# A Fourier and gated-MLP block on one core: the first 512 rows of x and of their DFT blocks loaded in another token order

## The chip, the cores and the metric

The kernel runs on one core of a Trainium2 chip. TensorE (PE) multiplies matrices, VectorE (DVE), ScalarE (ACT) and GpSimd (POOL) work element by element, and SyncE (SP) mostly issues DMAs. ACT and POOL issue some as well. All share the core's 16 DMA engines. The metric is the time of one execution in microseconds (us), lower is better.

## The reference

x is 2048 tokens by 512 features. Only the first half matters for the change: a normalization of x, and a two-dimensional discrete Fourier transform written as products with given cosine and sine matrices, of which the real part is kept. Everything is float32.

```python
h = _layernorm(x, axis=-1) * (1 + ca) + sa
a = jnp.einsum("bsd,ed->bse", h, dft_hid_re)
b = jnp.einsum("bsd,ed->bse", h, dft_hid_im)
y = jnp.einsum("ts,bse->bte", dft_seq_re, a) - jnp.einsum("ts,bse->bte", dft_seq_im, b)
x = x + ga * y
h = _layernorm(x, axis=-1) * (1 + cb) + sb
x = x + gb * _B_ref(h, ...)        # gelu, layernorm, a product over tokens, a gate, an output product
```

## The kernel before

A float32 product is made of three fast products. Each operand is split into a high part and a low part (`ah` and `al` for the DFT, `hh` and `hl` for the normalized x). ACT writes the high part, DVE the difference, and PE multiplies high by high, high by low and low by high into one accumulator.

The first phase takes the sum over the tokens s of the sequence DFT before the product with the hidden DFT. It runs 128 steps, numbered n, of 12 matmuls (128x512) each. A step contracts 128 tokens: its weights are the four 128-column chunks of one tile of normalized x, its moving operand is T[n], a 128x512 tile that has tokens on the partitions and DFT rows t on the columns. The DFT matrices are cut into 32 blocks of 512x512 (`src`). Four steps share a block. For the first 512 rows t the blocks alternate between cosine and sine (n 0 to 3 cosine, 4 to 7 sine, on the same four x tiles). Row group g means tokens 512g to 512g+511, held as four tiles in `XG[g]`.

A block arrives in the buffer `stage` (two buffers) with DFT rows on the partitions. `squares` (L190) makes T[n] of it with DVE's transpose of 32x32 squares. Such a transpose moves a token only within its 32, so `load_block` (L155) puts four pieces of 128 columns on the four quarters of the partitions, one DMA of 32 partitions and 256 KB for each. Tile k of a row group thus consists of the tokens 128a + 32k + i (a = 0 to 3, i = 0 to 31), and x is loaded in that same order by four DMAs of 32 partitions.

Later steps run ahead by a plan: before step n, `prep(n)` makes T[n+3] and its high part, and the low part of step n+2. When a block's last T is made, the block after the next is loaded into its buffer. `at(n, f)` runs f after step n. SP issues nearly all loads in program order, and each DMA waits for the DMA eight before it in the ring of eight completion semaphores.

The start is written out by hand, and the change lies there:

- `keep_busy` (L369) gives PE three matmuls on constants (six recorded passes), so that it works from 1.5 us on.
- `load_two` and `load_half` load x tiles 0 and 1 and the first 64 columns of each quarter of block 0 (T[0] and T[1]), on SP and ACT at once. `load_x` and `load_half` bring x tiles 2 and 3 and the other 64 columns on SP, and `load(1)` the sine block.
- Step 0 multiplies unsplit float32 (`whole_first` makes `xn`, `turn_whole` T[0], L543). It reads the four chunks in the order 1, 2, 3, 0.
- Steps 1 to 3 (L549) need `hh` (L483), `ah` (L269), `al` (L287) and `hl` (L525). `stats_first` (L439 to L445) gives the statistics on DVE and POOL. `norm_x` (L121) writes the float32 x from which `hl` is made.
- T has two buffers: T[2] takes the place of T[0], which PE reads until step 0 ends.
- Step 4 is the first with the plan's order (L97, L98, L99 for high-high, high by `al`, `hl` by high).

Of the kernel before, what the change touches and what calls it, by code (L numbers as in the profile page):

```python
# [20 lines left out]
def fnet_gmlp_kernel(  # L21
# [32 lines left out]
    nc = tc.nc  # L54
    S, D = x.shape[1:]
    F2 = w_in.shape[1]
    FH = F2 // 2
    Q = 512
    NQ = S // Q
# [73 lines left out]
    def quad(a, r, k):  # L133
        return a[r * Q:(r + 1) * Q, k * Q:(k + 1) * Q]

    src = []
    for t in range(NQ):
        for g, j in ([(g, j) for g in range(NQ) for j in range(2)] if t == 0 else
                     [(g, j) for j in range(2) for g in range(NQ)]):
            src.append(quad((cr, ci)[j], t, g))  # L140
    N2 = 4 * len(src)
    N1 = N2 + 8
    YPROD = (6, 7, 4, 5, 3)
# [8 lines left out]
    def load_block(tile_, a, s0=0, s1=P):  # L152
        v = a.rearrange("(b j) (a s) -> a j b s", j=32, a=4)
        for q in range(4):
            nc.sync.dma_start(tile_[32 * q:32 * q + 32, :, s0:s1], v[q][:, :, s0:s1])  # L155

    def load_half(tile_, a, h, engs=(nc.sync,) * 4):

        v = a.rearrange("(b j) (a s) -> a j b s", j=32, a=4)
        for q in range(4):  # L160
            engs[q].dma_start(tile_[32 * q:32 * q + 32], v[q][:, :, 64 * h:64 * h + 64])

    XB = []

    def load(b):
        if b < len(src):
            stage[b] = blocks.tile([P, 16, P], F32, tag="stage", bufs=2, name=f"stage{b}")
            load_block(stage[b], src[b])
        elif b < len(src) + 2:
            j = b - len(src)  # L170
            XB.append(blocks.tile([P, 4, Q], F32, tag="stage", bufs=2, name=f"xb{j}"))
            for g in range(2):
                nc.sync.dma_start(XB[j][:, 2 * g:2 * g + 2], ht_d[g].rearrange("(k p) t -> p k t", p=P)[:, 2 * j:2 * j + 2])
                for kk in range(2):
                    TT[2 * j + kk, g] = XB[j][:, 2 * g + kk]
# [13 lines left out]
    def squares(dst, block, k):  # L189
        nc.vector.transpose(dst.rearrange("p (b i) -> p b i", i=32), block[:, :, 32 * k:32 * k + 32])  # L190
# [61 lines left out]
    def prep_hi(n):  # L252
        if n >= NE or n in highs:
            return
        highs.add(n)
        if N2 <= n < N4:
            T[n] = form_t(n)
        else:
            b, k = divmod(n, 4) if n < N2 else (NB0 + (n - N4) // 4, (n - N4) % 4)
            if b != NB0:  # L260
                T[n] = blocks.tile([P, Q], F32, tag="t", bufs=2, name=f"t{n}")
            if b == NB0:
                assert n in T
            elif n >= N4:
                squares(T[n], stage[b][:, k % 2], k // 2)
            else:
                squares(T[n], stage[b], k)
        AH[n] = SE[2][:, n - N4] if N4 <= n < N4 + 4 else blocks.tile([P, Q], F32R, tag="ah", bufs=4, name=f"ah{n}")
        nc.scalar.activation(AH[n], T[n], AF.Copy)  # L269
        if not N2 <= n < N4 and k == 3:  # L270
            stage.pop(b)
            if b != NB0:
                load(b + 2)


# [89 lines left out]
    def keep_busy(n, k):  # L365

        ps = bank(k, "busyp")
        for _ in range(n):
            nc.tensor.matmul(ps, ones, busy, start=True, stop=True)  # L369

    def fold_sum(t, w, u):

# [46 lines left out]

    X, XG, LN, NRM, h_hi, h_lo = {}, {}, {}, {}, {}, {}  # L420

    def load_x(g, ks=range(4), eng=nc.sync):

        if g not in XG:
            XG[g] = spool.tile([P, 4, D], F32, tag="x", bufs=2, name=f"x{g}")
        k0, k1 = ks[0], ks[-1] + 1
        v = x.rearrange("(g a k i) d -> g a i k d", g=NQ, a=4, i=32)
        for a in range(4):
            eng.dma_start(XG[g][32 * a:32 * a + 32, k0:k1, :], v[g, a][:, k0:k1, :])
        for k in ks:  # L430
            X[4 * g + k] = XG[g][:, k, :]

# [2 lines left out]

    def stats_first(s):

        m = spool.tile([P, 12], F32, tag="first", bufs=4, name=f"first{s}")
        nc.vector.bn_stats(m[:, :6], X[s])  # L439
        mv = m[:, 8:]  # L440
        nc.vector.bn_aggr(mv[:, :2], m[:, :6])
        nc.vector.tensor_scalar(mv[:, 1:2], mv[:, 1:2], EPS, None, op0=ALU.add)
        nc.gpsimd.tensor_tensor(mv[:, 2:3], mv[:, 1:2], mhalf, op=ALU.pow)
        eng = nc.gpsimd if s else nc.vector
        eng.tensor_scalar(mv[:, 3:4], mv[:, 0:1], mv[:, 2:3], -1.0, op0=ALU.mult, op1=ALU.mult)  # L445
        NRM[s] = mv[:, 2:3], mv[:, 3:4]

    two = (nc.sync, nc.sync, nc.scalar, nc.scalar)

    def load_two(k):  # L450
        if not k:
            XG[0] = spool.tile([P, 4, D], F32, tag="x", bufs=2, name="x0")
        v = x.rearrange("(g a k i) d -> g a i k d", g=NQ, a=4, i=32)
        for a in range(4):
            two[a].dma_start(XG[0][32 * a:32 * a + 32, k, :], v[0, a][:, k, :])
        X[k] = XG[0][:, k, :]

    def whole_first(s):

        LN[s] = spool.tile([P, D], F32, tag="xn", bufs=4, name=f"xn{s}")  # L460
        nc.scalar.activation(LN[s].rearrange("p (k a i) -> p k a i", a=4, i=32),
                             X[s].rearrange("p (a k i) -> p k a i", a=4, i=32), AF.Identity,
                             bias=NRM[s][1], scale=NRM[s][0])
        nc.scalar.activation(LN[s][:, :1], ones[:, :1], AF.Copy)

    def split_first(s):
# [6 lines left out]

    def turn_whole(n):
        T[n] = blocks.tile([P, Q], F32, tag="t", bufs=2, name=f"t{n}")
        squares(T[n], stage[0], n)
        highs.add(n)
        lows.add(n)

    def hi_first(s):  # L480
        h_hi[s] = hpool.tile([P, ND, P], F32R, name=f"hh{s}")
        h = h_hi[s].rearrange("p k (a i) -> p k a i", i=32)
        nc.scalar.activation(h, X[s].rearrange("p (a k i) -> p k a i", a=4, i=32), AF.Identity,  # L483
                             bias=NRM[s][1], scale=NRM[s][0])
        nc.scalar.activation(h_hi[s][:, 0, :1], ones[:, :1], AF.Copy)
# [20 lines left out]
    def norm_x(s):  # L506

        if s not in LN:
            ones_x(s)
        elif s > 3:  # L510
            nc.gpsimd.memset(LN[s][:, 0:1], 1.0)
        apply(LN[s][:, 1:], X.pop(s)[:, 1:], NRM.pop(s))
# [9 lines left out]
    def lo_h(s):  # L522
        h_lo[s] = hpool.tile([P, ND, P], F32R, name=f"hl{s}")
        lo, h = parts_h(s, h_lo)
        nc.vector.tensor_tensor(lo, h, parts_h(s, h_hi)[0].bitcast(F32), op=ALU.subtract)  # L525
        LN.pop(s)
# [557 lines left out]
            mm([n])  # L1084


    load_two(0)
    stage[0] = blocks.tile([P, 16, P], F32, tag="stage", bufs=2, name="stage0")
    load_half(stage[0][:, :, :64], src[0], 0, two)
    load_two(1)  # L1090
    nc.scalar.activation(sc, ones[:, :ND], AF.Silu)
    load_x(0, range(2, 4))
    load_half(stage[0][:, :, 64:], src[0], 1)
    load(1)
    load_x(1, range(2))
    keep_busy(3, 5)
    ones_x(1)
    ones_x(2)
    ones_x(3)
    stats_first(0)  # L1100
    whole_first(0)
    turn_whole(0)
    prep_hi(1)
    stats_first(1)
    prep_lo(1)
    hi_first(1)
    stats_first(2)
    norm_x(1)
    stats_first(3)
    hi_first(2)  # L1110
    lo_h(1)
    prep_hi(2)
    norm_x(2)
    prep_hi(3)
    prep_lo(2)
    lo_h(2)
    hi_first(3)
    norm_x(3)
    prep_lo(3)
    split_first(0)  # L1120
# [11 lines left out]
    for s, n in ((4, 4), (5, 4), (6, 6), (7, 6), (8, 10), (9, 10)):  # L1132
        m = n + (s == 9)
# [316 lines left out]
```

## Time and profile before

| | |
|---|---|
| median of 3 runs | 931.55 us (931.38 to 931.88) |
| the profiled execution | 931.77 us |
| its span from first to last instruction | 930.0 us |
| PE busy | 924.2 us, 99% of the span |
| DVE, ACT, POOL busy | 738.2, 409.1, 199.1 us |
| moved by DMA | 157.88 MB, mean 170 GB/s |
| granted TensorE clock, mean | 0.999 |

A timeline row gives the start, the duration, the engine, the line, what is written from what, the count, and in brackets the idle time just before it and what ended that. Rows of several instructions are merged. Ends of matmuls are modelled, so starts are the better guide. "SPq" rows are the issuing of DMAs by SP.

### The profile page before, as it was taken

What the parts mean: (1) busy time and instruction counts of PE and PEld (TensorE: products, weight loads), DVE (VectorE), ACT (ScalarE), POOL (GpSimd) and SP (SyncE); (2) the same over time, 40 slices, a digit from 0 to 9 for tenths busy, and PEclk for the clock granted to TensorE, in tenths of its full rate; (3) what the DMA queues carried; (4) which work ended last, traced back from release to release, by engine and by line L of the source; (5) the groups of instructions that cost most, each with busy time, mean ns of one, the idle gap of its engine ahead of it and who ended that gap; (6) DMA issues with size and microseconds to landing.
All of it is one profiled execution on the core that took longest, in us unless ns stands there. A gap on an engine that the chain in (4) does not pass through costs nothing.

```text
span 930.0 us, 12339 instructions
## 1 busy us (share of the span) xinstructions
PE 924.2 (99%) x4053; PEld 760.4 (82%) x4053; DVE 738.2 (79%) x1218; ACT 409.1 (44%) x733; POOL 199.1 (21%) x375
## 2 busy tenths in 40 slices
PE   9999999999999999999999999999999999999998
PEld 5888888888888888888888888888888888888887
DVE  7799968787687677875678788899799789986762
ACT  5694424232132222322577877674544544331121
POOL 2330000224554165323512321331000000000000
PEclk9999999999999999999999999999999999999999
DMA  9995762856639977996463864444464566734651
GB/s 218 225 227 118 142 158 46 193 147 171 158 91 319 283 220 217 275 343 227 141 217 130 279 201 103 118 105 105 105 146 102 130 142 143 178 97 149 185 178 57
DMA packets 246976, 157.88 MB, mean 170 GB/s; under 512 B 140384, under 2 KB 214368, under 8 KB 246784
## 3 DMA queue, kind: packets, MB, share of 16 engines
q1 hardware_dynamic: 233248, 119.57, 52.2%
q0 software_dynamic: 12272, 36.86, 11.4%
q8 instruction: 32, 0.52, 0.2%
q10 hardware_dynamic: 1392, 0.66, 0.2%
q14 instruction: 32, 0.26, 0.1%
HBM read 120.33 MB, written 36.71 MB: 169 GB/s over the span
## 4 chain that ended last, share of the span: by engine, by line
PE 98%; DMA 1%; SPq 0%; ACTq 0%; DVE 0%; ACT 0%; issue 0%; DVEq 0%
PE gp L99 12%; PE gp L97 12%; PE gp L98 12%; PE gw L99 10%; PE gw L97 10%; PE gw L98 10%; PE yp L99 3%; PE yp L98 3%; PE yp L97 3%; PE op L98 3%; PE op L97 3%; PE op L99 3%; PE fp L98 1%; PE fp L97 1%; PE fp L99 1%; PE z2s L98 1%
## 5 line engine op out<-in xcount | busy, mean ns | idle before, releaser
L269 ACT ACTIVATE ah<-t 128x512 fp32r<-128x512 f32 x235 | 148.5, 632 | 362.6 <-DVE t L190 242.7
L287 DVE TENSOR_TENSOR al<-t,ah 128x512 fp32r<-128x512 f32 x235 | 160.6, 683 | 55.7 <-PE gp L98 30.9
L98 PE MATMUL gp<-al,hh 128*128 128x512 f32 x496 | 193.0, 389 | 0.0
L97 PE MATMUL gp<-ah,hh 128*128 128x512 f32 x496 | 193.0, 389 | 0.0
L99 PE MATMUL gp<-ah,hl 128*128 128x512 f32 x496 | 193.0, 389 | 0.0
L190 DVE STREAM_TRANSPOSE t<-stage 128x512 f32<-128x512 f32 x236 | 165.5, 702 | 6.3 <-DMA stage<-in_A_dft_seq_re_dram 3.1
L98 PE MATMUL gw<-al,bh 128*128 128x512 f32 x400 | 155.6, 389 | 0.0
L99 PE MATMUL gw<-ah,bl 128*128 128x512 f32 x384 | 149.5, 389 | 0.0
L97 PE MATMUL gw<-ah,bh 128*128 128x512 f32 x384 | 149.4, 389 | 0.0
L98 PEld LDWEIGHTS gp<-al,hh 128*128 128x128 f32 x496 | 93.1, 188 | 19.5 <-DVE al L287 0.2
L97 PEld LDWEIGHTS gp<-ah,hh 128*128 128x128 f32 x496 | 93.1, 188 | 19.4
L99 PEld LDWEIGHTS gp<-ah,hl 128*128 128x128 f32 x496 | 93.1, 188 | 19.3
L98 PEld LDWEIGHTS gw<-al,bh 128*128 128x128 f32 x400 | 75.1, 188 | 15.7
L99 PEld LDWEIGHTS gw<-ah,bl 128*128 128x128 f32 x384 | 72.1, 188 | 15.3 <-DVE bl L948 0.3
L97 PEld LDWEIGHTS gw<-ah,bh 128*128 128x128 f32 x384 | 72.1, 188 | 14.9
L920 POOL DMA_DIRECT2D s_d<-sj x64 | 35.1, 548 | 107.2 <-DVE sj L912 82.3
L97 PE MATMUL yp<-hth,gh 128*128 128x512 f32 x128 | 49.8, 389 | 0.0
L98 PE MATMUL yp<-htl,gh 128*128 128x512 f32 x128 | 49.8, 389 | 0.0
L99 PE MATMUL yp<-hth,gl 128*128 128x512 f32 x128 | 49.8, 389 | 0.0
L665 POOL DMA_DIRECT2D ht_d<-hturn x62 | 41.0, 667 | 23.1 <-DVE hturn L661 18.2
L97 PE MATMUL op<-woh,uh 128*128 128x512 f32 x110 | 42.8, 389 | 0.0
L98 PE MATMUL op<-wol,uh 128*128 128x512 f32 x110 | 42.8, 389 | 0.0
(247 smaller groups left out, 1449.4 us busy)
## 6 DMA issues: line engine op xcount, KB each, us to landing
stage<-in_A_dft_seq_im_dram SPq DMA_DIRECT2D x64, 256.0 KB, 6.0
sj<-in_B_w_sp_dram SPq DMA_DIRECT2D x32, 512.0 KB, 7.2
s_d<-sj POOLq DMA_DIRECT2D x64, 256.0 KB, 4.7
stage<-s_d SPq DMA_DIRECT2D x128, 128.0 KB, 2.9
stage<-in_A_dft_seq_re_dram SPq DMA_DIRECT2D x60, 256.0 KB, 5.6
stage<-in_B_w_sp_dram SPq DMA_DIRECT2D x88, 128.0 KB, 3.0
wm<-in_w_mod_dram SPq DMA_DIRECT2D x16, 256.0 KB, 6.1
xr<-in_A_x_dram POOLq DMA_DIRECT2D x16, 256.0 KB, 4.5
```

Source lines behind the costliest of these rows:

```text
L97: nc.tensor.matmul(acc, ah, bh, start=first, stop=False, skip_group_check=go_on)
L98: nc.tensor.matmul(acc, ah, bl, start=False, stop=False, skip_group_check=go_on)
L99: nc.tensor.matmul(acc, al, bh, start=False, stop=last, skip_group_check=go_on)
L190: nc.vector.transpose(dst.rearrange("p (b i) -> p b i", i=32), block[:, :, 32 * k:32 * k + 32])
L269: nc.scalar.activation(AH[n], T[n], AF.Copy)
L287: nc.vector.tensor_tensor(AL[n], t, AH[n].bitcast(F32), op=ALU.subtract)
L665: eng.dma_start(v[a, i], ht[32 * a:32 * a + 32].rearrange("c (b r) -> c b r", r=32))
L920: nc.gpsimd.dma_start(s_d[m, r, g][b * P:(b + 1) * P, :], a)
```

## The change

Row group 0 gets another token order. Tiles 0 and 1 are tokens 0 to 127 and 128 to 255 in their own order: x for each is one DMA of 128 partitions and 256 KB. Tiles 2 and 3 are the even and odd tokens of 256 to 511: x for both is one DMA of 512 KB, 4 KB for each partition.

The DFT blocks whose columns are row group 0 (8 of the 32) follow. For each of tiles 0 and 1, `load_row_of` issues four DMAs of 64 KB, in pieces of 32 columns, 128 bytes. For tiles 2 and 3 together `load_pair` issues four DMAs of 128 KB in pieces of 256 bytes. Such a block takes 12 DMAs where it took 4. `turn_dft` transposes tiles 2 and 3 from every second column. The other 24 blocks and row groups keep their loads.

At the start ACT now issues four DMAs, quarters 2 and 3 of the pieces for T[0] and T[1]. `keep_busy` does the same three matmuls. `whole_first` is two ACT instructions, chunks 1 and 2 and then 0 and 3, and the last statistics step of tile 0 moves from DVE to POOL. The calls after it stand in another order.

```diff
+    def load_row_of(tile_, a, k, qs=range(4), eng=nc.sync):
+        v = a[:, k * P:(k + 1) * P].rearrange("(b j) (a s) -> a j b s", j=32, a=4)
+        for q in qs:
+            eng.dma_start(tile_[32 * q:32 * q + 32, :, 32 * k:32 * k + 32], v[q])
+
+    def load_pair(tile_, a):
+        v = a[:, 2 * P:].rearrange("(b j) (a s) -> a j b s", j=32, a=4)
+        for q in range(4):
+            nc.sync.dma_start(tile_[32 * q:32 * q + 32, :, 64:], v[q])
+
+    def turn_dft(n, block, k, bs=slice(0, 16)):
+        t = T[n].rearrange("p (b i) -> p b i", i=32)
+        if SRC_G[n // 4] or k < 2:
+            nc.vector.transpose(t[:, bs, :], block[:, bs, 32 * k:32 * k + 32])
+        else:
+            v = block.rearrange("p b (h i c) -> p b h i c", h=2, c=2)
+            nc.vector.transpose(t[:, bs, :], v[:, bs, 1, :, k - 2])
...
-            load_block(stage[b], src[b])
+            if SRC_G[b]:
+                load_block(stage[b], src[b])
+            else:
+                load_row_of(stage[b], src[b], 0)
+                load_row_of(stage[b], src[b], 1)
+                load_pair(stage[b], src[b])
...
+        if not g:
+            if k0 < 2:
+                nc.sync.dma_start(XG[g][:, k0, :], x[k0 * P:(k0 + 1) * P, :])
+            else:
+                nc.sync.dma_start(XG[g][:, 2:, :], x[2 * P:Q, :].rearrange("(p k) d -> p k d", k=2))
...
-    load_two(0)
+    load_x(0, range(1))
     stage[0] = blocks.tile([P, 16, P], F32, tag="stage", bufs=2, name="stage0")
-    load_half(stage[0][:, :, :64], src[0], 0, two)
-    load_two(1)
+    load_row_of(stage[0], src[0], 0, range(2))
+    load_row_of(stage[0], src[0], 0, range(2, 4), nc.scalar)
+    load_x(0, range(1, 2))
+    load_row_of(stage[0], src[0], 1, range(2, 4), nc.scalar)
+    load_row_of(stage[0], src[0], 1, range(2))
     nc.scalar.activation(sc, ones[:, :ND], AF.Silu)
     load_x(0, range(2, 4))
-    load_half(stage[0][:, :, 64:], src[0], 1)
+    load_pair(stage[0], src[0])
...
-    keep_busy(3, 5)
+    keep_busy((Q, Q, Q), 5)
...
     turn_whole(0)
+    stats_first(1)
     prep_hi(1)
-    stats_first(1)
-    prep_lo(1)
     hi_first(1)
     stats_first(2)
+    prep_lo(1)
     norm_x(1)
+    hi_first(2)
+    prep_hi(2)
+    lo_h(1)
     stats_first(3)
-    hi_first(2)
-    lo_h(1)
-    prep_hi(2)
     norm_x(2)
+    prep_lo(2)
     prep_hi(3)
-    prep_lo(2)
+    hi_first(3)
     lo_h(2)
-    hi_first(3)
     norm_x(3)
     prep_lo(3)
```

The order on DVE before, from the statistics of x tile 2 to the second transpose of block 1. `t_225` and `t_230` are T[2] and T[3], `t_268` is T[4], `al_239` the low part of step 2, `hl_223` that of x tile 1:

```order
L439 BN_STATS first_207<-x_138 128x6
...
L439 BN_STATS first_214<-x_138 128x6
L441 BN_AGGR first_214<-first_214 128x2
L442 TENSOR_SCALAR first_214<-first_214 128x1
L525 TENSOR_TENSOR hl_223<-xn_175,hh_204 128x512
L190 STREAM_TRANSPOSE t_225<-stage_143 128x512
L190 STREAM_TRANSPOSE t_230<-stage_143 128x512
L287 TENSOR_TENSOR al_239<-t_225,ah_227 128x512
L525 TENSOR_TENSOR hl_241<-xn_177,hh_220 128x512
L287 TENSOR_TENSOR al_247<-t_230,ah_232 128x512
L525 TENSOR_TENSOR hl_253<-xn_179,hh_243 128x512
L190 STREAM_TRANSPOSE t_268<-stage_161 128x512
```

The same place now, where `t_221` and `t_236` are T[2] and T[3], `hl_225` the low part of x tile 1 and `t_272` is T[4]:

```order
L314 TENSOR_TENSOR al_215<-t_202,ah_204 128x512
L183 STREAM_TRANSPOSE t_221<-stage_140 128x512
L560 TENSOR_TENSOR hl_225<-xn_178,hh_206 128x512
L476 BN_STATS first_227<-x_138 128x6
L481 BN_AGGR first_227<-first_227 128x2
L482 TENSOR_SCALAR first_227<-first_227 128x1
L314 TENSOR_TENSOR al_234<-t_221,ah_223 128x512
L183 STREAM_TRANSPOSE t_236<-stage_140 128x512
L560 TENSOR_TENSOR hl_248<-xn_180,hh_218 128x512
L314 TENSOR_TENSOR al_251<-t_236,ah_238 128x512
L560 TENSOR_TENSOR hl_257<-xn_182,hh_245 128x512
L180 STREAM_TRANSPOSE t_272<-stage_156 128x512
```

T[2] now stands ahead of `hl` of tile 1 and of the statistics of tile 3, and T[3] no longer follows T[2] directly: four kinds of work lie between them.

SP's queue before, down to the first ordinary block (`stage_143` is block 0, `stage_161` block 1, `stage_234` block 2):

```order
L455 DMA x_138<-in_A_x_dram 32x512 x2
L161 DMA stage_143<-in_A_dft_seq_re_dram 32x16x64 x2
L455 DMA x_138<-in_A_x_dram 32x512 x2
L429 DMA x_138<-in_A_x_dram 32x2x512 x4
L161 DMA stage_143<-in_A_dft_seq_re_dram 32x16x64 x4
L155 DMA stage_161<-in_A_dft_seq_im_dram 32x16x128 x4
L429 DMA x_166<-in_A_x_dram 32x2x512 x4
L155 DMA stage_234<-in_A_dft_seq_re_dram 32x16x128 x4
```

And now (`stage_140`, `stage_156` and `stage_240` are blocks 0, 1 and 2):

```order
L456 DMA x_138<-in_A_x_dram 128x512
L168 DMA stage_140<-in_A_dft_seq_re_dram 32x16x32 x2
L456 DMA x_138<-in_A_x_dram 128x512
L168 DMA stage_140<-in_A_dft_seq_re_dram 32x16x32 x2
L458 DMA x_138<-in_A_x_dram 128x1024
L174 DMA stage_140<-in_A_dft_seq_re_dram 32x16x64 x4
L168 DMA stage_156<-in_A_dft_seq_im_dram 32x16x32 x8
L174 DMA stage_156<-in_A_dft_seq_im_dram 32x16x64 x4
L462 DMA x_169<-in_A_x_dram 32x2x512 x4
L156 DMA stage_240<-in_A_dft_seq_re_dram 32x16x128 x4
```

Ahead of the last DMA for T[2] and T[3] SP issued 13 DMAs, now 10. Block 1 behind it took 4 and takes 12.

## Rows read from the trace of the kernel before

**Rows 1.** The page's first part: busy time, share of the span, instructions.
```profile
PE 924.2 (99%) x4053; PEld 760.4 (82%) x4053; DVE 738.2 (79%) x1218; ACT 409.1 (44%) x733; POOL 199.1 (21%) x375
```
**Rows 2.** Waits of PE over the whole span: total us, times, longest.
```profile
PE busyp L369 <- DVE busy L308: 1.5, 1, 1.5
PE gp L549 <- ACT ah L269: 0.7, 1, 0.7
```
**Rows 3.** Timeline of PE, start to step 4; columns as told above.
```profile
1.53 5.46 PE L369 MATMUL busyp<-busy,ones 128*128 128x512 f32 x6 [1.53 <-DVE busy L308]
...
5.93 1.06 PE L369 MATMUL busyp<-busy,ones 128*128 128x512 f32 x1
6.82 3.85 PE L543 MATMUL gp<-t,xn 128*128 128x512 f32 x8
10.52 1.19 PE L549 MATMUL gp<-ah,hh 128*128 128x512 f32 x4
...
14.26 1.20 PE L549 MATMUL gp<-ah,hh 128*128 128x512 f32 x4 [0.72 <-ACT ah L269]
...
19.85 0.39 PE L97 MATMUL gp<-ah,hh 128*128 128x512 f32 x1
20.08 0.39 PE L98 MATMUL gp<-al,hh 128*128 128x512 f32 x1
```
**Rows 4.** The chain of waits, one step of it near the start.
```profile
8.40 4.31 DMA stage<-in_A_dft_seq_re_dram
```
**Rows 5.** Timeline of DVE, 9 to 20 us.
```profile
9.31 0.69 DVE L439 BATCH_NORM_STATS2 first<-x 128x6 f32<-128x512 f32 x1 [0.47 <-DMA x<-in_A_x_dram]
...
10.33 0.68 DVE L439 BATCH_NORM_STATS2 first<-x 128x6 f32<-128x512 f32 x1
...
12.83 1.30 DVE L190 STREAM_TRANSPOSE t<-stage 128x512 f32<-128x512 f32 x2 [0.69 <-DMA stage<-in_A_dft_seq_re_dram]
...
17.12 0.69 DVE L525 TENSOR_TENSOR hl<-xn,hh 128x512 fp32r<-128x512 f32 x1 [0.88 <-ACT xn L121]
17.72 1.30 DVE L190 STREAM_TRANSPOSE t<-stage 128x512 f32<-128x512 f32 x2
19.13 0.69 DVE L287 TENSOR_TENSOR al<-t,ah 128x512 fp32r<-128x512 f32 x1
```
**Rows 6.** Timeline of ACT, 14 to 19 us.
```profile
14.82 0.61 ACT L269 ACTIVATE ah<-t 128x512 fp32r<-128x512 f32 x1
...
18.46 1.28 ACT L269 ACTIVATE ah<-t 128x512 fp32r<-128x512 f32 x2 [0.86 <-DVE t L190]
```
**Rows 7.** Timeline of SP, the issues of DMAs, 4 to 9 us.
```profile
4.84 1.98 SPq L429 DMA_DIRECT2D x<-in_A_x_dram  x4
6.86 2.02 SPq L161 DMA_DIRECT2D stage<-in_A_dft_seq_re_dram  x4
```
**Rows 8.** DMA view, issues from 0.7 to 1.1 us: count, size, us to landing.
```profile
x<-in_A_x_dram ACTq DMA_DIRECT2D x1, 64.0 KB, 2.2
x<-in_A_x_dram SPq DMA_DIRECT2D x1, 64.0 KB, 2.0
```
**Rows 9.** DMA view, packets of three stretches: 868.2:870.8, 8.3:11.0, 48.1:53.5.
```profile
DMA packets 2312, 0.64 MB, mean 245 GB/s; under 512 B 2129, under 2 KB 2129, under 8 KB 2312
DMA packets 2135, 0.58 MB, mean 215 GB/s; under 512 B 2037, under 2 KB 2118, under 8 KB 2135
DMA packets 2211, 1.19 MB, mean 220 GB/s; under 512 B 76, under 2 KB 2154, under 8 KB 2210
```
**Rows 10.** Timelines of DVE and of PE where block 4 arrives.
```profile
46.10 0.71 DVE L190 STREAM_TRANSPOSE t<-stage 128x512 f32<-128x512 f32 x1 [2.36 <-DMA stage<-in_A_dft_seq_re_dram]
46.73 0.65 DVE L287 TENSOR_TENSOR al<-t,ah 128x512 fp32r<-128x512 f32 x1
...
49.81 0.39 PE L97 MATMUL gp<-ah,hh 128*128 128x512 f32 x1
50.03 0.39 PE L98 MATMUL gp<-al,hh 128*128 128x512 f32 x1
```
**Rows 11.** Busy time by stretch: length, PE, PEld, DVE, ACT, POOL, clock, DMA share, GB/s.
```profile
46.00:56.00 10.00, 10.00 (x46) 8.29 (x45) 9.02 (x15) 9.01 (x21) 2.21 (x7) 1.00 1.19 223
...
76.00:86.00 10.00, 10.00 (x46) 8.29 (x45) 8.24 (x14) 6.36 (x14) 1.31 (x2) 1.00 0.57 128
```

More of the change, by code (lines that the diff above doesn't have):

```diff
@@ L134, in quad @@
         return a[r * Q:(r + 1) * Q, k * Q:(k + 1) * Q]
-    src = []
+    src, SRC_G = [], []
     for t in range(NQ):
@@ L140, in fnet_gmlp_kernel @@
             src.append(quad((cr, ci)[j], t, g))
+            SRC_G.append(g)
     N2 = 4 * len(src)
@@ L266, in prep_hi @@
             else:
-                squares(T[n], stage[b], k)
+                turn_dft(n, stage[b], k)
         AH[n] = SE[2][:, n - N4] if N4 <= n < N4 + 4 else blocks.tile([P, Q], F32R, tag="ah", bufs=4, name=f"ah{n}")
@@ L367, in keep_busy @@
         ps = bank(k, "busyp")
-        for _ in range(n):
-            nc.tensor.matmul(ps, ones, busy, start=True, stop=True)
+        for w in n:
+            nc.tensor.matmul(ps[:, :w], ones, busy[:, :w], start=True, stop=True)
     def fold_sum(t, w, u):
@@ L420, in fnet_gmlp_kernel, with load_x @@
     X, XG, LN, NRM, h_hi, h_lo = {}, {}, {}, {}, {}, {}
-    def load_x(g, ks=range(4), eng=nc.sync):
+    def load_x(g, ks=range(4)):
         if g not in XG:
@@ L426, in load_x @@
         k0, k1 = ks[0], ks[-1] + 1
-        v = x.rearrange("(g a k i) d -> g a i k d", g=NQ, a=4, i=32)
-        for a in range(4):
-            eng.dma_start(XG[g][32 * a:32 * a + 32, k0:k1, :], v[g, a][:, k0:k1, :])
+        if not g:
[3 more added lines that the diff above has]
+                nc.sync.dma_start(XG[g][:, 2:, :], x[2 * P:Q, :].rearrange("(p k) d -> p k d", k=2))
+        else:
+            v = x.rearrange("(g a k i) d -> g a i k d", g=NQ, a=4, i=32)
+            for a in range(4):
+                nc.sync.dma_start(XG[g][32 * a:32 * a + 32, k0:k1, :], v[g, a][:, k0:k1, :])
         for k in ks:
@@ L436, in stats_first, with sums_first, norm_first, halves @@
     def stats_first(s):
[L438 to L441, printed above, removed]
+        sums_first(s)
+        norm_first(s)
+    def sums_first(s):
+        M1[s] = spool.tile([P, 12], F32, tag="first", bufs=4, name=f"first{s}")
+        nc.vector.bn_stats(M1[s][:, :6], X[s])
+    def norm_first(s):
+        mv = M1[s][:, 8:]
+        nc.vector.bn_aggr(mv[:, :2], M1[s][:, :6])
         nc.vector.tensor_scalar(mv[:, 1:2], mv[:, 1:2], EPS, None, op0=ALU.add)
         nc.gpsimd.tensor_tensor(mv[:, 2:3], mv[:, 1:2], mhalf, op=ALU.pow)
-        eng = nc.gpsimd if s else nc.vector
-        eng.tensor_scalar(mv[:, 3:4], mv[:, 0:1], mv[:, 2:3], -1.0, op0=ALU.mult, op1=ALU.mult)
+        nc.gpsimd.tensor_scalar(mv[:, 3:4], mv[:, 0:1], mv[:, 2:3], -1.0, op0=ALU.mult, op1=ALU.mult)
         NRM[s] = mv[:, 2:3], mv[:, 3:4]
[L448 to L456, printed above, removed]
+    M1 = {}
+    def halves(h, s):
+        v = X[s].rearrange("p (a k i) -> p k a i", a=4, i=32)
+        for ks in (slice(1, 3), slice(0, 4, 3)):
+            nc.scalar.activation(h[:, ks], v[:, ks], AF.Identity, bias=NRM[s][1], scale=NRM[s][0])
     def whole_first(s):
         LN[s] = spool.tile([P, D], F32, tag="xn", bufs=4, name=f"xn{s}")
-        nc.scalar.activation(LN[s].rearrange("p (k a i) -> p k a i", a=4, i=32),
-                             X[s].rearrange("p (a k i) -> p k a i", a=4, i=32), AF.Identity,
-                             bias=NRM[s][1], scale=NRM[s][0])
+        halves(LN[s].rearrange("p (k a i) -> p k a i", a=4, i=32), s)
         nc.scalar.activation(LN[s][:, :1], ones[:, :1], AF.Copy)
@@ L475, in turn_whole @@
         T[n] = blocks.tile([P, Q], F32, tag="t", bufs=2, name=f"t{n}")
-        squares(T[n], stage[0], n)
+        turn_dft(n, stage[0], n)
         highs.add(n)
```

## The prediction

> **What bounds the kernel now.** I read the busy times first: PE works 99% of the span [rows 1]. The waits of PE come next, because with a full PE only its idle time and its own work can change. It waits twice: 1.5 us for the constants before the first matmul, and 0.72 us at the first product of step 2 [rows 2]. The change takes no matmul away. So I looked at the first 20 us of PE: six passes on constants from 1.53, step 0 at 6.82, step 1 at 10.52, step 2 at 14.26 after the idle time, step 4 at 19.85 [rows 3]. After step 4 PE never waits, so the end of the kernel follows the start of step 4 one for one, as long as nothing new stops PE later. The question is when step 4 can start.
>
> Step 2's idle time ends a chain: the last DMA of block 0's second half goes out at 8.40 and takes 4.31 us to land [rows 4], the transposes T[2] and T[3] start at 12.83 after a DMA wait [rows 5], and ACT's high part follows. What holds step 4 is the same chain further on: `hl` of tile 3 (17.12), T[4] and T[5] (17.72), the low part `al` of step 4 (19.13, 0.69 long) [rows 5]. PE reads that at 20.08 [rows 3]. It is done at 19.82, so this chain has only about 0.2 us of room. A gain before step 4 counts only as far as this `al` comes earlier too.
>
> **The first matmul: nothing to speak of.** x tile 0 and T[0] should be ready earlier, with half as many bytes of block 0 ahead of T[0]. But PE is on constants until then: the last of the six passes starts at 5.93 and a pass takes (5.93 - 1.53) / 5 = 0.88 us [rows 3], so they end at about 6.8, where step 0 starts now. `keep_busy` keeps its three matmuls. Weights loaded ahead of time could give 0.1 to 0.2 us here, which does not reach step 4 if the chain above sets it. The two ACT halves and the step moved to POOL lie inside this cover. A cost shows only if T[0] or the first half comes after 6.8.
>
> **The DMAs for T[2] and T[3].** SP spends 1.98 / 4 and 2.02 / 4 us on an issue [rows 7], 0.5 us. Before, 13 DMAs stood ahead of the last one, and four of them started only at 4.84. Now 10 stand ahead. Four go out by about 2.7, the fifth waits for ACT's first DMA (issued near 0.7, 64 KB, 2.2 us to landing [rows 8]), that is to about 3.1, and six more issues of 0.5 us put the last one at 6.1 to 6.4 instead of 8.40. With the landing time of 4.31 us [rows 4] it is there at 10.4 to 10.7. The other way round: 2.1 MB must have come by then, as before, and at 215 to 245 GB/s [rows 9] that takes 8.6 to 9.8 us from about 2 us, 10.6 to 11.8. I take 10.7, and T[2] at 10.8. It can't be before about 10.5, because T[2] takes T[0]'s buffer and PE reads that until step 0 ends (10.52 [rows 3]). The late end is 12.83, as before.
>
> **The chain behind T[2].** The new order on DVE puts work between T[2] and T[3]: T[2] itself 0.65 (half of the 1.30 of two), `hl` of tile 1 0.70, the statistics of tile 3 10.33 - 9.31 = 1.02, `al` of step 2 0.70 [rows 5]. T[3] starts 3.07 us after T[2], where it was 0.65. ACT's high part of T follows a transpose by 18.46 - 17.72 = 0.74 [rows 5, 6], and from ACT's high part of step 3 to `al` of step 4 it takes 19.13 - 14.82 = 4.31 [rows 5, 6]: the same instructions in the same order. So `al` of step 4 starts at T[2] + 3.07 + 0.74 + 4.31 = T[2] + 8.12. It was free to start at 20.08 - 0.69 - 0.06 = 19.33 without holding PE. Nothing is gained if T[2] starts at 11.2, and each us earlier or later moves the end by one us. T[2] at 10.8 gives **0.4 us**. At 10.5 it gives 0.7, at 12.83 it costs 1.6. PE's own work would allow more, step 0 to 3 without idle time end near 18.6, but the chain doesn't. On the way step 1 needs `hl` of tile 1 some 1.95 us after its start (12.4), which stands behind T[2] on DVE now: T[2] at 10.8 has it ready at 12.15.
>
> T[2], T[3] and the same tiles of later blocks are read from every second column. No row shows a transpose with such a step. The nearest are those from whole runs of 32, 0.65 to 0.70 us [rows 5]. A double price, 1.4 as an estimate, would put 0.7 on each of T[2] and T[3] and 1.4 on step 4. I take no surcharge, since the count of elements is the same, and keep the other end for the range.
> The Trainium skill, page "SBUF — State Buffer", section "Door 1: The DMA port swizzle", says that accesses within one 16-byte line run at full rate, so that four-byte elements may lie some apart for free. By that the step of 8 bytes costs nothing and the sum stays 0.4. No row here shows it.
>
> **Blocks loaded in small pieces.** Block 1 goes from 2048 pieces of 512 bytes to 4096 of 128 and 2048 of 256. In the stretch 868.2:870.8 a late load of this kernel moved some 2048 pieces of 128 bytes in 2.6 us, in 8.3:11.0 the pair loads moved about 2048 of 256 bytes in 2.7, in 48.1:53.5 about 2080 of 512 bytes took 5.4 [rows 9]. So the block takes 2 x 2.6 + 2.7 = 7.9 us of the queue instead of about 5.3, 2.6 more. It starts about 2 us earlier, behind a last pair at 10.7 instead of 12.7. Every transfer behind it moves by +0.6 us, by +2.6 if the pair comes no earlier. The DMA engines are full from then to past 56 us (223 GB/s at a share over 1 [rows 11]), so the shift is not made good. It meets DVE at 46.10, where T[16] already waits 2.36 us for block 4 [rows 10]. Behind T[16] stands `al` of step 15, done at 46.73 + 0.65 = 47.38, and PE reads it at 50.03 [rows 10]. The cover is 2.65 us, or 2.25 with PE 0.4 us ahead. A shift of 0.6 costs nothing. The six later blocks of this kind meet DMA engines at a share of 0.57 [rows 11] and cost nothing. SP's 12 issues for one are 6 us against a block's four steps of 2.7 us. What waits behind them on SP has the same room.
>
> **Sum.** 931.77 of the profiled execution less 0.4 is 931.4. That execution is 0.2 above the median of the runs, so 931.2 against 931.55.
>
> **Rivals.**
> - *The gap only moves.* T[2] starts between 10.9 and 11.6, step 2 waits less and step 4 waits for its `al`: 931.3 to 932.0. For it: the second way of estimating the landing (10.6 to 11.8). Chance 0.25.
> - *T[2] as late as before.* The pair loads land near 12.7, or the transposes with a step cost double: step 4 is 1.4 to 1.6 us later, 933.1. Against it: the issues are two us earlier. It decides from T[2] = 11.2 on. Chance 0.09.
> - *The small pieces reach PE.* Block 4 lands more than 2.65 us later than before and `al` of step 15 holds PE. A shift of 4 us costs 1.35: 932.9. For it: the stretch of rows 9 with 128 bytes read rows that lie together, the DFT rows lie 8 KB apart. Against it: 256-byte pieces of those rows ran at 2.7 us per 2048. Chance 0.10.
> The Trainium skill, page "DMA: Bandwidth & Descriptors", section "Specifications", asks for 512 bytes or more for full rate, which speaks against this change. Rows 9 agree per byte: 128-byte pieces move at some 105 GB/s.
> - *The chain is shorter than I think.* DVE reaches `al` of step 4 early and PE runs steps 0 to 3 through, step 4 at 18.6: 930.3. Against it: five DVE steps of row 5 stand in it. Chance 0.08.
>
> My forecast, 930.8 to 931.4, has the remaining 0.48. Without the outer halves of the two slow rivals the range is 930.4 to 932.6.
>
> A measurement of this kernel can tell about 0.2%, 1.9 us. PE's whole idle time that could go is below that, so faster gets 0.02. Slower gets the far parts of two rivals, 0.07. The rest is within 0.2%.
>
> **What would show it.** Right: no idle time of PE before step 2, T[2] near 10.8, T[3] three us behind it, step 4 near 19.4, `al` of step 4 the last to come there, T[16] waiting some 0.6 us longer than 2.36, and no wait of PE at step 15. Wrong: step 0 later than 6.9, T[2] after 11.5, a strided transpose over 0.8 us, or a PE wait after 20 us.

## The result and the profile after

The changed kernel took **934.43 us** (median, 932.93 to 937.08) against 931.54 of the kernel before in the same comparison. The ratio is 1.0037, with a 95% interval of 1.0029 to 1.0045. It is slower, by about 2.9 us, and outside the predicted range. The profiled execution took 936.22 us with a span of 934.4, against 931.77 and 930.0, so the two profiles show more of a loss (4.4 us) than the medians.

Which steps of the start lost it is read from PE's waits (engine, line, what it waited for: total us, times, longest), which answer to [rows 2]:

```profile
PE gp L584 <- DVE al L314: 1.6, 1, 1.6
PE busyp L396 <- DVE busy L335: 1.5, 1, 1.5
PE gp L97 <- DVE gl L93: 1.3, 1, 1.3
PE gp L584 <- ACT ah L296: 0.5, 1, 0.5
PE gp L98 <- DVE al L314: 0.2, 1, 0.2
```

The wait for `ah` at step 2, 0.7 us before, is now 0.5 us, and three waits have come that before didn't have. Of these four only the one for `gl` lies behind the first 23 us. The timeline of PE there, to be held against [rows 3]:

```profile
10.27 1.50 PE L584 MATMUL gp<-ah,hh 128*128 128x512 f32 x4
...
13.38 1.20 PE L584 MATMUL gp<-al,hh 128*128 128x512 f32 x4 [1.61 <-DVE al L314]
...
16.26 1.20 PE L584 MATMUL gp<-ah,hh 128*128 128x512 f32 x4 [0.46 <-ACT ah L296]
...
22.73 0.50 PE L98 MATMUL gp<-al,hh 128*128 128x512 f32 x1 [0.23 <-DVE al L314]
```

The product with `al` of step 4 starts at 22.73, where it was 20.08: 2.65 us lost at the start. The fourth wait is far behind it:

```profile
319.49 0.50 PE L97 MATMUL gp<-ah,hh 128*128 128x512 f32 x1 [1.29 <-DVE gl L93]
```

Both kernels run the same 4053 recorded matmuls. Set side by side by their number, the changed kernel is 2.65 us behind from step 4 on, 4.2 us behind after the wait at 319.49, and 4.39 at the end. So there are two losses, one at the start and one at 319 us, and nothing else of size.

**The start, on DVE** (to be held against [rows 5]):

```profile
11.63 0.69 DVE L476 BATCH_NORM_STATS2 first<-x 128x6 f32<-128x512 f32 x1 [3.16 <-DMA x<-in_A_x_dram]
...
12.64 0.68 DVE L314 TENSOR_TENSOR al<-t,ah 128x512 fp32r<-128x512 f32 x1
13.24 0.70 DVE L183 STREAM_TRANSPOSE t<-stage 128x512 f32<-128x512 f32 x1
...
16.24 0.69 DVE L314 TENSOR_TENSOR al<-t,ah 128x512 fp32r<-128x512 f32 x1 [0.68 <-ACT ah L296]
16.85 0.71 DVE L183 STREAM_TRANSPOSE t<-stage 128x512 f32<-128x512 f32 x1
...
21.98 0.69 DVE L314 TENSOR_TENSOR al<-t,ah 128x512 fp32r<-128x512 f32 x1
```

DVE stands 3.16 us for x tiles 2 and 3, which come in one DMA issued at 5.16. Behind that wait, in DVE's order, stand `al` of step 1 (12.64), for which PE waits 1.61 us, and T[2] (13.24). T[2] was forecast for 10.8. But DVE's order is not what made it that late. Of the four DMAs that bring T[2]'s and T[3]'s own data, the last went out at 7.2 and took 5.6 us to land (DMA view of the stretch 7.4:7.7: count, size, us to landing), so it was there at 12.8:

```profile
stage<-in_A_dft_seq_re_dram SPq DMA_DIRECT2D x1, 128.0 KB, 5.6
```

**The late wait.** SP's issues there, first before, then after (start, us, line, destination, count):

```profile
290.96 2.03 SPq L155 DMA_DIRECT2D stage<-in_A_dft_seq_re_dram  x4
295.55 1.20 SPq L907 DMA_DIRECT2D sj<-in_B_w_sp_dram  x2
```
```profile
293.70 6.08 SPq L168 DMA_DIRECT2D stage<-in_A_dft_seq_re_dram  x8
299.82 2.31 SPq L174 DMA_DIRECT2D stage<-in_A_dft_seq_re_dram  x4
302.31 1.72 SPq L942 DMA_DIRECT2D sj<-in_B_w_sp_dram  x2
```

This is block 24, one of the six later blocks in small pieces. Behind it on SP stands a load of `sj` in two DMAs of 512 KB, parts of the second phase's weight `w_sp` that DVE sums for later use. It went out 4.6 us behind the start of block 24's issues before, and now 8.6 us behind. DVE's timeline, before and then after:

```profile
306.42 0.69 DVE L912 TENSOR_TENSOR sj<-sj 128x512 f32<-128x512 f32 x1
...
312.72 2.73 DVE L93 TENSOR_TENSOR gl<-gp,gh 128x512 fp32r<-128x512 f32 x4 [0.78 <-ACT gh L92]
```
```profile
312.91 0.69 DVE L947 TENSOR_TENSOR sj<-sj 128x512 f32<-128x512 f32 x1 [3.66 <-DMA sj<-in_B_w_sp_dram]
...
318.74 2.49 DVE L93 TENSOR_TENSOR gl<-gp,gh 128x512 fp32r<-128x512 f32 x4 [0.69 <-ACT gh L92]
```

The sum had no wait before. Now DVE stands 3.66 us for a sum that could wait (experiment 4), and its later work is late with it, down to `gl`, the low part of the finished token product. Before, the first of the four parts of `gl` was made by about 313.4, and PE read it at 315.29:

```profile
315.29 0.39 PE L97 MATMUL gp<-ah,hh 128*128 128x512 f32 x1
```

`gl` now comes 6.0 us later than before. Some 2.7 of that is the lag from the start, 1.9 was room at PE, and the rest is the wait of 1.29.

### The profile page after: what moved, and what is told of

Same layout as the page of the kernel before. It is cut to its first block, busy times and chain, and to the rows that moved or that the text cites. A ratio compares the mean times of both kernels' runs of the same rounds, so it can differ in the third digit from the quotient of the medians.

```text
span 934.4 us, 12413 instructions
## 1 busy us (share of the span) xinstructions
PE 925.7 (99%) x4053; PEld 760.2 (81%) x4053; DVE 736.8 (79%) x1217; ACT 408.6 (44%) x734; POOL 200.5 (21%) x376
## 3 DMA queue, kind: packets, MB, share of 16 engines
q0 software_dynamic: 12272, 36.86, 11.2%
## 4 chain that ended last, share of the span: by engine, by line
PE 95%; SPq 2%; DMA 2%; DVE 1%; issue 0%; ACT 0%; DVEq 0%; ACTq 0%
PE gp L98 11%; PE gp L97 11%; PE gp L99 11%; PE gw L98 10%; PE gw L99 10%; PE gw L97 10%; PE yp L99 3%; PE yp L98 3%; PE yp L97 3%; PE op L98 3%; PE op L97 3%; PE op L99 3%; PE fp L98 1%; PE fp L97 1%; PE fp L99 1%; DMA stage<-in_A_dft_seq_re_dram 1%
## 5 line engine op out<-in xcount | busy, mean ns | idle before, releaser
L180 DVE STREAM_TRANSPOSE t<-stage 128x512 f32<-128x512 f32 x112 | 78.3, 699 | 6.0 <-DMA stage<-in_A_dft_seq_re_dram 3.2
L217 DVE STREAM_TRANSPOSE t<-stage 128x512 f32<-128x512 f32 x108 | 76.2, 705 | 2.2 <-DMA stage<-in_B_w_sp_dram 1.2
```

The costliest lines, as they stand in the source:

```text
L180: nc.vector.transpose(t[:, bs, :], block[:, bs, 32 * k:32 * k + 32])
```

## The experiments

Theory: two separate losses, as above, both of them work that stands in an engine's order behind a late DMA. Against it stand "only DVE's order at the start", "only the landing of x", "the small pieces cost everywhere they are used", "twelve issues are too many for SP" and "the 128-byte pieces fill the queue at the start".

**1. The start alone, two ways.** In `after_order` the calls for `al`, `xn` and `hl` of step 1 stand ahead of the statistics of x tile 2:

```
     hi_first(1)
-    stats_first(2)
     prep_lo(1)
     norm_x(1)
+    lo_h(1)
+    stats_first(2)
```

> The changed kernel with one edit in the order of calls: the low part of step 1 and the low part of x tile 1 stand ahead of the statistics of x tile 2 on VectorE. Theory 1 (x tiles 2 and 3 land at about 11.5 us, and VectorE waited 3.16 us for them with the low part of step 1 queued behind): the 1.61 us wait of TensorE inside step 1 goes, step 2 starts at 14.5 to 14.8 instead of 16.26, and the median falls by 1.0 to 1.6 us, from 934.4 to about 933. Rival (the wait only moves to the chain of step 4, since T[2] still stands behind the statistics): step 4 starts as late as 22.7 and the median stays at 934.4.

Measured: 935.41 us, ratio 1.0043 (1.0030 to 1.0057). PE's wait in step 1 is gone, and step 2 waits 2.24 us for `ah`. The wait only moves, as the rival said: the chain of T[2] decides when the `al` product of step 4 starts (22.14 us). The DMAs for T[2] had landed at 11.9 here, and T[2] began at 13.04, behind the work put ahead of it on DVE.

In `after_x4` x tiles 2 and 3 come by four DMAs of 128 KB instead of one:

```
-                nc.sync.dma_start(XG[g][:, 2:, :], x[2 * P:Q, :].rearrange("(p k) d -> p k d", k=2))
+                v = x[2 * P:Q, :].rearrange("(a i k) d -> a i k d", a=4, k=2)
+                for a in range(4):
+                    nc.sync.dma_start(XG[g][32 * a:32 * a + 32, 2:, :], v[a])
```

> The changed kernel with x tiles 2 and 3 in four DMAs of 128 KB (32 partitions each) instead of one of 512 KB, in the same token order. Theory 1a (a single DMA of 128 partitions is held by the slowest of the 16 engines, the form is at fault): the tiles land near 9.3 us as before, VectorE waits for them under 1 us instead of 3.16, the median falls by 1.5 to 2.5 us. Rival 1b (the lag comes from all that was sent before, whatever the form): they land at 11 to 12 and the median stays at 934.4, or rises by the 1.5 us of three more issues.

Measured: 934.38 us, 1.0041 (1.0028 to 1.0055). x is there 1.7 us earlier (statistics of tile 2 at 9.94), T[2] at 12.50, and step 4's `al` product at 21.32. This start is better by 1.4 us, but the end is no earlier: at 319 us PE waited 2.5 us for `gl`, and the granted clock was 0.51 from 319 to 321 us and 0.63 from 321 to 323. (The profile is of the longest of the five runs.) So the start isn't all of it.

**2. The small pieces without the new start.** Both kernels are the kernel before, where `load_block` is called three times for a block, with the first 32, the next 32 and the last 64 columns of each quarter: 12 DMAs with the piece sizes of the change. `block1_pieces` does so for block 1, `late_pieces` for blocks 8, 12, 16, 20, 24 and 28.

```
-            load_block(stage[b], src[b])
+            if b == 1:            # late_pieces: b >= 8 and b % 4 == 0
+                load_block(stage[b], src[b], 0, 32)
+                load_block(stage[b], src[b], 32, 64)
+                load_block(stage[b], src[b], 64, P)
+            else:
+                load_block(stage[b], src[b])
```

> The kernel before, with block 1 alone loaded in pieces of 128, 128 and 256 bytes, 12 DMAs. By the working of the prediction the queue runs 2.6 us later from there on, VectorE's wait for block 4 grows from 2.36 to about 5 us, the cover of 2.65 us holds just about, and the time stays at 931.5 (931.3 to 932.3). Rival (the small pieces reach TensorE): a wait of TensorE at step 15 of 0.5 us or more, 932.3 to 934.

Measured: 932.48 us, 1.0010 (1.0002 to 1.0019). At step 15 PE doesn't wait. It waits 1.2 us for `xn` ahead of step 0, because its constants ended earlier in this execution (step 0 starts at 6.93 all the same), and 0.6 us for `hl` near 31 us. DVE and then PE:

```profile
25.24 0.71 DVE L195 STREAM_TRANSPOSE t<-stage 128x512 f32<-128x512 f32 x1 [1.83 <-DMA stage<-in_A_dft_seq_re_dram]
```
```profile
31.29 0.50 PE L99 MATMUL gp<-ah,hl 128*128 128x512 f32 x1 [0.60 <-DVE hl L530]
```

DVE stands 1.83 us for block 2, which is queued behind block 1 on SP and went out at 17.42 instead of 14.16. `hl` follows in DVE's order. Up to there PE is 0.69 us ahead of the profile of before (experiment 4 says why), after it 0.07 us behind. So the small pieces of block 1 do reach PE, by way of block 2 and not of block 4. Another 0.5 us goes near 807 us, where nothing was changed.

> The kernel before, with the six later blocks of row group 0 (blocks 8, 12, 16, 20, 24, 28) loaded in pieces of 128, 128 and 256 bytes, 12 DMAs each. Theory 2 (the 12 DMAs hold up SyncE's queue and the loads of w_sp behind them, and VectorE waits for those, 3.66 us near 312 us in the changed kernel): a wait of TensorE of 0.5 to 1.5 us near 315 us, the median 932.0 to 933.0. The prediction's step (these blocks cost nothing): 931.5.

Measured: 934.36 us, 1.0035 (1.0019 to 1.0051). The old start with the six late blocks loses as much as the whole change. DVE waits 5.23 us for `sj` at 311.10, and PE:

```profile
317.66 0.80 PE L97 MATMUL gp<-ah,hh 128*128 128x512 f32 x1 [2.48 <-DVE gl L93]
318.26 0.63 PE L98 MATMUL gp<-al,hh 128*128 128x512 f32 x1
...
320.94 0.40 PE L99 MATMUL gp<-ah,hl 128*128 128x512 f32 x1
```

**3. Which block, and what in it.** `late_24` does it for block 24 alone (`if b == 24` in the diff above). `late_24_rows` also loads block 24 by 12 DMAs, but cut by rows, so that each piece is still 512 bytes:

```
+            if b == 24:
+                for b0, b1 in ((0, 4), (4, 8), (8, 16)):
+                    load_rows(stage[b], src[b], b0, b1)   # v[q][:, b0:b1] of load_block
```

> The kernel before, with block 24 alone in twelve transfers of small pieces (rows of 128, 128 and 256 bytes); its columns keep their order. Theory L (the load of sj that stands behind block 24 on SP comes late, VectorE waits for it, the new token matmuls wait for VectorE): the whole loss of the six late blocks is here, 934 us (933 to 936), VectorE waits 3 to 5 us for sj near 311 us, TensorE 1.3 to 2.5 us for gl near 318 us. Rival M (each of the six blocks costs its share): a sixth of 3 us, 931.8 us, and no wait for sj of over 1 us.

Measured: 933.95 us, 1.0035 (1.0022 to 1.0049). One block of 32 costs 2.6 us. The waits of PE and the row of DVE:

```profile
PE gp L97 <- DVE gl L93: 2.0, 1, 2.0
```
```profile
310.10 0.69 DVE L917 TENSOR_TENSOR sj<-sj 128x512 f32<-128x512 f32 x1 [4.41 <-DMA sj<-in_B_w_sp_dram]
```

> The kernel before, with block 24 in twelve transfers too, but cut by rows, so that every piece is still 512 bytes. Theory P (the small pieces hold the queues): the time of before, 931.3 us, no wait for sj of over 0.5 us near 311 us. Rival C (twelve issues where there were four: SP's own time, 12 x 0.6 = 7 us, and its ring of semaphores put the load of sj off): 933 to 935 us, with the load of sj issued some 5 us later than in before (295.6 us) and the wait of 3 us or more at VectorE.

Measured: 931.78 us, 1.0004 (0.9994 to 1.0013). This is not to be told from before in the median. But the profiled execution, at 932.76 the longest of its runs, shows the same pattern, 3.69 us at DVE and 1.3 at PE. So twelve issues alone can make the load of `sj` late enough in an execution, though not in the median. With the small pieces even the shortest run (933.17) is longer than any of before (932.09). The two parts are not separated further than that.

**4. Take the wait away and leave all the DMAs.** `after_sum_late` is the changed kernel, `late_sum_late` is `late_pieces`, both with the sums of that one load of `sj` two steps later:

```
-    when = ([(82 + 4 * i, 3) for i in range(11)] +
+    when = ([(82 + 4 * i, 5 if i == 2 else 3) for i in range(11)] +
```

> The kernel before with the six late blocks in small pieces, and the same edit of the sums. Theory L: the time of before, 931.3 us (930.9 to 931.9), no wait of TensorE for gl of over 0.5 us near 318 us. Rival M (the small pieces cost elsewhere too): 932.5 us or more, with the waits of TensorE spread over the six blocks.

Measured: 931.39 us, 0.9999 (0.9990 to 1.0008). All of the loss of `late_pieces` is gone, with every small piece still there. That settles the late part: by themselves the late small pieces cost nothing that this comparison can tell (at most 0.8 us), and the wait of DVE at that sum was the price.

> The changed kernel, with one edit: the two sums of the third sj load (issued at step 90) stand at steps 95 and 96 and not at 93 and 94, so that VectorE comes to them some 6 us later. Theory L: the wait for sj near 312 us is gone, and with it 1.6 to 2.4 us of the loss; what the start lost (2.65 us at step 4 in the profile, of which some is the start's own spread) stays: 932.3 us (931.6 to 933.2). Rival S (the start alone sets the loss, the late wait eats cover): 934 us as the changed kernel. Rival G (the start gains once the late loss is out): under 931.

Measured: 933.24 us, 1.0018 (1.0009 to 1.0027). PE has no wait after step 4:

```profile
PE busyp L396 <- DVE busy L335: 1.5, 1, 1.5
PE gp L584 <- DVE al L314: 0.6, 1, 0.6
PE gp L584 <- ACT ah L296: 0.6, 1, 0.6
PE gp L98 <- DVE al L314: 0.2, 1, 0.2
```

What is left, 1.9 us, is the start. In this profile PE is 1.38 us behind the profile of before at step 4 and 1.5 at the end. That profile of before was itself late at its start: step 2 began at 14.26, behind the wait of 0.72 us [rows 2]. Five kernels have the very same start (`block1_pieces`, `late_pieces`, `late_24`, `late_24_rows`, `late_sum_late`). In none of their profiles is that wait there: T[2] starts at 12.03 to 12.40, step 2 at 13.45 to 13.82 and the `al` product of step 4 at 19.25 to 19.65, where the profile of before has 20.08. DVE and then PE of `late_24`:

```profile
12.03 1.30 DVE L195 STREAM_TRANSPOSE t<-stage 128x512 f32<-128x512 f32 x2
```
```profile
13.45 1.19 PE L554 MATMUL gp<-ah,hh 128*128 128x512 f32 x4
...
19.25 0.40 PE L98 MATMUL gp<-al,hh 128*128 128x512 f32 x1
```

So medians show some 0.5 us more than the two profiles.

**5. What sets the start.** All three have the late sums too. `start_256` keeps the new start's issues and bytes, but the eight DMAs for T[0] and T[1] bring pieces of 256 bytes (so its result is another one). In `ah_first` the high part of T[2] stands ahead of `hh` of tile 2 on ACT. `ah_first_x2` does that, puts `al` of step 1 ahead of the statistics of tile 2, and loads x tiles 2 and 3 by a DMA each.

```
     stats_first(2)
     prep_lo(1)
     norm_x(1)
-    hi_first(2)
     prep_hi(2)
+    hi_first(2)
     lo_h(1)
```

> The changed kernel with the late sums as in after_sum_late, and block 0's first eight transfers in pieces of 256 bytes: the same 64 KB each and the same issues, but each brings 8 of the 16 row groups and 64 columns of the quarter, so T[0] and T[1] hold other columns of the matrix (the result of steps 0 and 1 is another one). Theory Z (the pieces of 128 bytes take the queue ahead of x tiles 2 and 3): these land near 9 us and not 10.2, T[2] starts near 10.6, step 4 at 20 us or before, and the time is 931.3 to 932.0. Theory D (DVE's order sets the start: T[2] stands behind the statistics of tile 2 and al of step 1, step 2's high part behind hh on ACT): x tiles 2 and 3 land within 0.4 us of 10.2 and the time is that of after_sum_late, 932.6 to 933.8.

Measured: 933.69 us, 1.0022 (1.0012 to 1.0033). x tiles 2 and 3 are there at 10.49 (10.30 with 128-byte pieces), and ACT's first DMA of 64 KB took 3.7 us to land (3.5). The theory of the small pieces falls for these eight DMAs.

```profile
10.49 0.69 DVE L486 BATCH_NORM_STATS2 first<-x 128x6 f32<-128x512 f32 x1 [2.45 <-DMA x<-in_A_x_dram]
```

> The changed kernel with the late sums, and on ACT the high part of T[2] ahead of hh of tile 2 (it stood behind it, and hh waits for the statistics of tile 2). Theory D: the high part ends near 13.2 us and not 14.9, DVE's al of step 2 no longer waits 0.76 us for it, and step 4 starts some 0.7 us earlier than in after_sum_late (21.46): 932.5 (931.8 to 933.2). Theory Z (the landing of x and of the pairs sets it): no change, 933.2.

Measured: 932.64 us, 1.0015 (1.0006 to 1.0024). By the median it is not separated from `after_sum_late`, whose interval overlaps. The profile does separate them. DVE and then PE:

```profile
11.74 0.71 DVE L183 STREAM_TRANSPOSE t<-stage 128x512 f32<-128x512 f32 x1 [0.51 <-DMA stage<-in_A_dft_seq_re_dram]
...
13.95 0.68 DVE L314 TENSOR_TENSOR al<-t,ah 128x512 fp32r<-128x512 f32 x1
...
19.81 0.69 DVE L314 TENSOR_TENSOR al<-t,ah 128x512 fp32r<-128x512 f32 x1
```
```profile
20.56 0.50 PE L98 MATMUL gp<-al,hh 128*128 128x512 f32 x1 [0.23 <-DVE al L314]
```

`al` of step 2 no longer waits, and step 4 is 0.48 us behind before instead of 1.38. T[2] now waits for its own DMA, as in the forecast, but at 11.74.

> As ah_first, with al of step 1 ahead of the statistics of tile 2 on DVE, and x tiles 2 and 3 in two transfers of 256 KB, one a tile, so that the statistics of tile 2 wait for half the bytes. Theory D: x tile 2 is there 1 us earlier than both were (9.2 for 10.2 us), al of step 1 and of step 2 hold nothing, step 4 starts at 20.0 to 20.5 us: 931.6 (931.0 to 932.3), equal to the kernel before. If one lagging DMA engine holds every landing back to 11 us or more whatever its size, no gain over ah_first: 932.5.

Measured: 932.65 us, 1.0017 (1.0008 to 1.0026). The statistics of tile 2 no longer wait (9.37), and T[2] starts at 11.83 behind its DMA. No gain over `ah_first`: once DVE and ACT hold nothing, the pair loads (the four DMAs for T[2] and T[3], the last landing at 11.7) set T[2]. No version beat the kernel before.

## Why the prediction was wrong

The bound was named rightly: PE is full, and the end follows step 4's `al` and any later wait. The form of the sum held too. It said that `al` of step 4 starts 8.12 us after T[2] and that T[2] at 11.2 is the break-even against the profile of before. With T[2] at t and a chain of c, the loss at step 4 should be (t - 11.2) + (c - 8.12):

| kernel | last pair load landed | T[2] starts | to `al` of step 4 | by the formula | measured at PE |
|---|---|---|---|---|---|
| changed | 12.8 | 13.24 | 8.74 | +2.66 | +2.65 |
| after_order | 11.9 | 13.04 | 8.35 | +2.07 | +2.06 |
| after_x4 | 12.3 | 12.50 | 8.07 | +1.25 | +1.24 |
| start_256 | 12.0 | 12.13 | 8.72 | +1.53 | +1.52 |
| after_sum_late | 11.7 | 11.91 | 8.80 | +1.39 | +1.38 |
| ah_first_x2 | 11.7 | 11.83 | 8.07 | +0.58 | +0.57 |
| ah_first | 11.6 | 11.74 | 8.07 | +0.49 | +0.48 |

As t + c is the start of that `al`, the agreement shows only that PE reads it as soon as it is made, in all seven. The columns show where the time goes. A transpose that waits for its DMA alone starts 0.1 us after the landing (12.71 and 12.83 before). So of the 2.65 us in the changed kernel the landing has 1.7, DVE's order 0.3 and the longer chain 0.6. Step by step:

- **The wait to be gained.** This step failed, and it took the gain with it. The 0.72 us at step 2 was taken from one execution; the five other profiles with this start don't have it. Against them the break-even for T[2] is 10.4 to 10.8 (19.25 to 19.65, less 0.75 and 8.12), not 11.2, and T[2] at 10.8 gains nothing. The 18.6 for PE's own work was low too: 19.85 less the 0.72 is 19.13, and step 4 begins at 19.03 to 19.41 there.
- **The first matmul.** Right: 6.89 for 6.82.
- **When the pair loads land (forecast 10.7).** Mis-sized, and the largest part of the loss at the start. SP's fifth issue waited for ACT's first DMA, as said, but that took 3.5 us and not the 2.2 of [rows 8], so the last pair went out at 7.2 instead of 6.1 to 6.4. With the 4.5 us that they then took (`ah_first`) T[2] can start at 11.74. That alone turns the gain of 0.4 into a loss of 0.5. In the changed kernel's profile they took 5.6 us, and it is 1.7. With the old start the last of these DMAs went out at 8.1 to 8.5 and landed at 11.3 to 12.0 in the five profiles, against 11.6 to 12.8 in the table above. So issuing them a microsecond earlier brought no earlier landing. The row taken was of a 64 KB DMA of x, in few large pieces. The other estimate in the text, by bytes, gave 10.6 to 11.8 and was the better one.
- **T[2] follows its DMA at once.** Not so, and the working has no line for it, but the price was small. On DVE the statistics of x tile 2 and `al` of step 1 stand ahead of T[2], 1.6 us of work, and they wait for x tiles 2 and 3, now a single DMA of 512 KB. The landing of that DMA was never estimated. It came at 11.6, and T[2]'s own at 12.8, so this order cost T[2] 0.3 us, and under 0.1 in `after_sum_late` and `start_256`.
- **The chain of 8.12.** The sum is right (8.07) where ACT does the high part of T[2] first, or where x tiles 2 and 3 are in early (`after_x4`). In the changed kernel `hh` of tile 2 stands ahead of it on ACT, and `al` of step 2 waits 0.68 us for that. The working looked at DVE's order only.
- **No surcharge for every second column.** Right: 0.70 and 0.71 us. The Trainium skill, page "SBUF — State Buffer", section "Door 1: The DMA port swizzle", which the prediction named for it, agrees with these rows.
- **Block 1 in small pieces.** Right where it looked: T[16] waits 2.9 us (forecast some 3), and PE doesn't wait at step 15. But the working followed the shift to block 4 alone, and block 2 stands right behind block 1. In `block1_pieces` that made PE wait 0.6 us, and the price is 0.2 to 1.8 us, where nothing was forecast. In the changed kernel PE, 2.7 us late by then, doesn't wait there.
- **The six later blocks cost nothing.** This step failed, and alone it costs the most (2.6 to 3.1 us; about 1 on top of the late start): "What waits behind them on SP has the same room." It hadn't. The sum needs the second of the two DMAs of `sj`. Before, that one went out at 296.1 and took 7.5 us, so it was there at 303.6, and its sum came at 306.42 (the row of before above): a room of 2.8 us. Against block 24's first issue the load went out 2.5 us later than before in `late_24_rows`, 3.6 in `late_24` and 4.0 in the changed kernel, and its second DMA then took 11.4, 8.8 and 9.4 us to land. Free DMA engines (a share of 0.57 [rows 11]) and a block's own room said nothing on this, and the stretch of rows 11 was another one: at 295 to 315 us the share was 1.1.

The rival of the small pieces had the right mechanism and the wrong place, block 4 instead of block 2 and the load behind block 24. "T[2] as late as before" (chance 0.09) came true at the start: the last pair load landed at 12.8, near its 12.7. No case had both losses together.

The Trainium skill, page "DMA: Bandwidth & Descriptors", section "Specifications", asks for pieces of 512 bytes or more for full rate. `late_24` against `late_24_rows` agrees (losses of 2.6 and 0.5 us by the medians), `start_256` shows no difference between 128 and 256.

What stays open: the two losses don't quite add in the medians. Late blocks alone cost 2.6 to 3.1 us and the start alone 1.9, while both cost 2.9. No run shows why the late one is smaller behind a late start. Nor did any run bring the pair loads in earlier, so what sets their landing stays open.

## What to carry to other kernels

When a load is split into more DMAs, list what is queued behind it on the same queue and, for each, the time between its landing and its first reader. Here that room counted, not the free share of the DMA engines. A load that is needed much later can still hold the kernel, when an engine that works in order reads it early. Moving that reader was cheap here: two steps gave back all of the 3 us of `late_pieces`.

When a step is said to start as soon as its DMA lands, write down every instruction ahead of it on its engine and the DMA of each.

Before a wait is priced, look for it in more than one execution. The 0.72 us to be gained here was in one profile of six.

## What was not expected of the hardware

**A long wait costs PE more than its length.** In `late_pieces`, after the 2.48 us, the matmuls followed each other 0.43 us apart instead of 0.23, for more than 2 us. The windows (length, PE, PEld, DVE, ACT, POOL, granted clock, DMA share, GB/s) show the clock at about half, the level of 1.2 GHz, and then back at 2.4:

```profile
317.00:319.00 2.00, 1.34 (x3) 1.15 (x4) 2.00 (x4) 1.34 (x3) 0.00 (x0) 0.54 1.02 406
319.00:321.00 2.00, 2.00 (x7) 1.53 (x7) 1.97 (x4) 0.63 (x1) 0.00 (x0) 0.61 0.18 70
321.00:323.00 2.00, 2.00 (x11) 1.64 (x10) 1.97 (x4) 0.63 (x1) 0.19 (x1) 1.00 0.56 166
```

PE's distance to before grew there by another 1.4 us, from 2.4 to 3.8. `after_x4` shows the same after 2.47 us. After the wait of 1.29 us in the changed kernel and of 2.0 in `late_24` the granted clock stayed at 1.00.

**A DMA can land long after most of its bytes.** In the changed kernel, with x tiles 2 and 3 still awaited, the stretch 10.5:11.5 moved almost nothing, and none of its packets has the 4 KB pieces of that DMA:

```profile
DMA packets 77, 0.02 MB, mean 18 GB/s; under 512 B 77, under 2 KB 77, under 8 KB 77
```

SP stood 3.17 us in one issue just before (7.76 to 10.93); for what, the profile doesn't show. The same DMA, issued at 5.10 to 5.16, took 4.4 us in `ah_first`, 5.2 in `after_sum_late` and 6.4 in the changed kernel. The runs of the changed kernel spread over 4.2 us, those of before in the same comparison over 0.7. This DMA is not the main reason: `late_pieces`, with the old start and the late wait, spreads over 6.5 us, and `after_sum_late`, with the new start and no late wait, over 2.1.
